# A recurrence's output written with its axes swapped, in strips of 32 columns

## The chip, the cores and the metric

The kernel runs on one core of a Trainium2 chip. The metric is the time of one execution on the device in microseconds; the number given for a kernel is the median of its runs. A core has a matmul engine (TensorE, PE in the rows; its weight loads are shown apart as PEld), a vector engine (VectorE, DVE), ScalarE (ACT), GpSimd (POOL), and SyncE (SP), which here only issues transfers. Each engine works through its own list of instructions in order and waits on semaphores of the others. Matmuls write to PSUM, from which DVE and ACT read.

## The reference

A linear recurrence runs per batch and head over 768 steps, with a state of 48 x 48; its output goes through two feed-forward layers.

```python
for t in range(S):                                  # B, H, S, D = 4, 8, 768, 48
    cur = np.einsum('bhd,bhe->bhde', u[None] * kt, vt)
    y[:, :, t] = np.einsum('bhd,bhde->bhe', rt, state + cur)
    state = wt[:, :, :, None] * state + np.einsum('bhd,bhe->bhde', kt, vt)
...
x = y.transpose(0, 2, 1, 3).reshape(B * S, H * D)    # 3072 x 384
h = x @ w_in                                         # 384 -> 2048
x = (h * np.clip(h + 3.0, 0.0, 6.0) / 6.0) @ w_out   # 2048 -> 384
out = ((x @ w1) * (x @ w2) @ w3) @ w_out2            # 384 -> 1024 -> 1024 -> 384
```

## The kernel before

The 768 steps are cut into six chunks of C = 128. A unit is one chunk of one batch, so there are 24 units, numbered uu = 4 * chunk + batch. Heads go in NP = 4 pairs: head 2 pr on partitions 0 to 47 and head 2 pr + 1 on partitions 64 to 111 (G = 112). All of a unit's products are f32 matmuls; the feed-forward matmuls (`mm3`, three per product: high by high, high by low, low by high) use f32r halves and 512 moving columns.

A unit's steps have one letter each, and the table ORDER is a list of them: `P12` is step P of unit 12. The steps that matter here:

- `P`, `F`: scans over w on DVE. `K` / `k`: k times a decay, on DVE / GpSimd. `R` / `r`: r times a decay, on DVE / GpSimd; both then load the next w.
- `n`, `m`: transposes of k (line 288) and their copy `kn`. `s`: the scores, 8 matmuls of 48 rows, by turns on partitions 0 to 47 and 64 to 111 (line 300). `a`, `b`: copies of the scores to `A` on ACT. `c`, `d`: the causal mask on GpSimd (line 311).
- The bonus, the term with u. First chunk: `q` (GpSimd, line 315) multiplies k and r, `e` (line 321) reduces over d with `ubk`, a 112 x 8 copy of u, and `w` (DVE, line 325) multiplies v by the result. Later chunks: `u`, `v`, `l`, and `w` on GpSimd (line 332). In both cases the product is written over r in the tile `nat`, which holds r, k, v of the unit in rows by time (`nr`, `nk`, `nv`).
- `T`, `t`, `y`: the state's decay, its matmuls (line 341: kn by 96 columns of v per pair) and the addition into `St`.
- `o`: the output (line 354). Per pair one matmul of r by the state (128 x 128 weights, 96 columns) and one per head of `A` by v (48 columns), into `py`, 128 time steps by 384 features.
- `x`: DVE adds the bonus to `py` into `x` (line 368). `f`: three transposes of `x` (line 374) into `px`, 384 features by 128 time steps. `g`, `h`: the high half `xh` on ACT and the low half `xl` on DVE, the operands of the feed-forward layer.

Letters without a number are the feed-forward layer and its weights: `G` and `B` are the matmuls into and out of the hidden layer (9 each), `E M H L` the work between them on ACT, DVE, ACT and GpSimd; `S a d i p` load a block of weights and split it (ACT and DVE), `V` stores; `D` is a dummy matmul, 128 x 256 in bf16, on no data of the problem. A block of the feed-forward layer takes 512 time steps, those of the four units of a chunk, and 16 times `G ... B`. ORDER covers five of the six blocks; the sixth, the fold of w3 into w_out2 and the second layer come after the last unit.

The first transfers stand in LO, in which `w0` is w of unit 0 and `n0` is its `nat`. SyncE issues them; LO1 says how many come before the other instructions of the start. `ubk` is loaded between them, by ScalarE's queue:

```python
for x in LO.split()[0:LO1]:
    LD[x[0]](int(x[1]))
nc.scalar.activation(out=ones, in_=ones, func=ACTF.Copy)
nc.scalar.dma_start(out=ubk[0:G], in_=uT)
```

## Time and profile before

| | us |
|---|---|
| median of 3 runs (907.05 to 911.94) | 910.64 |
| the profiled execution | 910.93 |
| its span, first to last instruction | 909.2 |
| PE busy in the span | 879.9 (97%) |
| DVE, ACT, POOL busy | 376.7, 328.5, 367.4 |

The times in the sections below are of the profiled execution, counted from the start of its span. A matmul's record runs from its start to the modelled end of its results; records of neighbours overlap, so what a matmul costs is read from one start to the next and not from its duration. An f32 matmul stands as two records. The granted clock (PEclk) is given as a share of full speed. "Idle before" is the time in which an engine waited ahead of an instruction, with what released it.

### The profile page before, as it was taken

How to read it: one execution, taken by the hardware profiler on the slowest of the kernel's cores; microseconds unless marked ns; L12 is line 12 of the kernel's file. 1: busy time of each engine (PE TensorE's matmuls, PEld its weight loads, DVE VectorE, ACT ScalarE, POOL GpSimd, SP SyncE). 2: the span in 40 equal slices, each digit the busy share in tenths (PEclk: the TensorE clock that was granted, in tenths of full speed). 3: DMA queues.
4: the chain of work that ended last, by engine and by line, in shares of the span. 5: the costliest groups of instructions: out<-in, count | busy, mean ns of one | idle time of the engine just before them, and what ended most of it. 6: DMA issues, size and time to landing. Idle time of an engine off the chain costs nothing. (4 is left out here: it accounts for less than half of the span.)

```text
span 909.2 us, 11518 instructions
## 1 busy us (share of the span) xinstructions
PE 879.9 (97%) x4534; PEld 731.6 (80%) x4534; DVE 376.7 (41%) x562; ACT 328.5 (36%) x556; POOL 367.4 (40%) x336
## 2 busy tenths in 40 slices
PE   5989999999999999999999999989999999999997
PEld 4978787888888888888888889868888888888785
DVE  5598997634256416544211444246211122112110
ACT  1356653333333333333223655365222222222211
POOL 5376674545546545655322310122323231322221
PEclk6799999999999999999999999999999999999999
DMA  7466531411122113112200445272020403030001
GB/s 211 150 206 196 178 131 58 128 56 59 46 79 81 57 56 93 57 57 82 73 1 1 145 164 165 82 246 73 0 90 1 151 1 132 20 104 28 35 1 39
DMA packets 29230, 80.20 MB, mean 88 GB/s; under 512 B 3312, under 2 KB 3952, under 8 KB 29168
## 3 DMA queue, kind: packets, MB, share of 16 engines
q1 hardware_dynamic: 29040, 79.38, 27.1%
q8 instruction: 38, 0.62, 0.3%
q14 instruction: 24, 0.20, 0.1%
q10 hardware_dynamic: 128, 0.00, 0.0%
HBM read 69.93 MB, written 9.44 MB: 87 GB/s over the span
## 5 line engine op out<-in xcount | busy, mean ns | idle before, releaser
L440 POOL TENSOR_TENSOR gl<-t,gh 128x512 fp32r<-128x512 f32 x144 | 188.7, 1310 | 421.4 <-ACT gh L436 415.6
L436 ACT ACTIVATE gh<-t 128x512 fp32r<-128x512 f32 x144 | 90.9, 632 | 201.6 <-DVE t L595 105.4
L595 DVE TENSOR_TENSOR t<-t,wk 128x512 f32<-128x512 f32 x48 | 32.9, 686 | 200.0 <-PE wk L183 200.0
L429 DVE SCALAR_TENSOR_TENSOR t<-t,h 128x512 f32<-128x512 f32 x96 | 65.4, 682 | 119.7 <-ACT t L424 119.2
L424 ACT ACTIVATE t<-h 128x512 f32<-128x512 f32 x96 | 57.0, 594 | 157.7 <-PE h L183 150.7
L181 PE MATMUL h<-xh,wioh 128*128 128x512 f32 x234 | 97.3, 416 | 0.0
L181 PE MATMUL acc<-gh,wioh 128*128 128x512 f32 x234 | 93.7, 401 | 0.0
L183 PE MATMUL h<-xh,wiol 128*128 128x512 f32 x234 | 92.7, 396 | 0.0
L182 PE MATMUL h<-xl,wioh 128*128 128x512 f32 x234 | 92.3, 394 | 0.0
L182 PE MATMUL acc<-gl,wioh 128*128 128x512 f32 x234 | 91.4, 391 | 0.7 <-POOL gl L440 0.7
L183 PE MATMUL acc<-gh,wiol 128*128 128x512 f32 x234 | 91.6, 391 | 0.0
L594 ACT ACTIVATE t<-h 128x512 f32<-128x512 f32 x48 | 28.6, 595 | 99.9 <-PE h L183 99.9
L182 PE MATMUL acc<-gl,w34h 128*128 128x512 f32 x144 | 56.3, 391 | 0.0
L183 PE MATMUL acc<-gh,w34l 128*128 128x512 f32 x144 | 56.3, 391 | 0.0
L181 PE MATMUL acc<-gh,w34h 128*128 128x512 f32 x144 | 56.2, 390 | 0.0
L362 PE MATMUL wk<-nat,A 128*128 128x48 f32 x384 | 54.9, 272 | 0.2 <-POOL A L311 0.2
L311 POOL TENSOR_SCALAR_AFFINE_SELECT A<-A 128x512 f32<-128x512 f32 x48 | 41.7, 891 | 29.2 <-ACT A L307 29.2
L183 PEld LDWEIGHTS h<-xh,wiol 128*128 128x128 f32 x234 | 44.2, 189 | 10.2
L181 PEld LDWEIGHTS h<-xh,wioh 128*128 128x128 f32 x234 | 44.4, 190 | 9.8 <-DVE t L429 0.3
L165 ACT ACTIVATE z<-st 128x768 f16<-128x768 bf16 (+2 forms) x46 | 41.2, 900 | 30.4 <-DVE st L169 11.7
L182 PEld LDWEIGHTS acc<-gl,wioh 128*128 128x128 f32 x234 | 44.1, 189 | 9.8 <-POOL gl L440 1.0
L183 PEld LDWEIGHTS acc<-gh,wiol 128*128 128x128 f32 x234 | 43.9, 188 | 9.8
(141 smaller groups left out, 1805.8 us busy)
## 6 DMA issues: line engine op xcount, KB each, us to landing
st<-in_wio_dram SPq DMA_DIRECT2D x16, 768.0 KB, 4.3
nat<-in_rkv_dram SPq DMA_DIRECT2D x20, 576.0 KB, 3.8
st<-in_w3T_dram SPq DMA_DIRECT2D x16, 512.0 KB, 4.2
W<-in_wT_dram SPq DMA_DIRECT2D x24, 224.0 KB, 2.7
K<-in_kT_dram SPq DMA_DIRECT2D x24, 224.0 KB, 2.6
R<-in_rT_dram SPq DMA_DIRECT2D x24, 224.0 KB, 2.6
st<-in_wT_dram SPq DMA_DIRECT2D x12, 448.0 KB, 6.6
x1d<-ev SPq DMA_DIRECT2D x18, 256.0 KB, 2.9
```

The source lines that it names most:

```text
L165: nc.scalar.activation(out=z.bitcast(FP16).rearrange("p (n two) -> p n two", two=2)[:, :, 1], in_=half, func=ACTF.Copy)
L181: nc.tensor.matmul(ps_ap, lh, rh, start=first, stop=False)
L182: nc.tensor.matmul(ps_ap, lh, rl, start=False, stop=False)
L183: nc.tensor.matmul(ps_ap, ll, rh, start=False, stop=last)
L311: nc.gpsimd.affine_select(out=A, in_=A, compare_op=ALU.is_ge, fill=0.0, base=-1, pattern=[[0, NP], [1, C]], channel_multiplier=-1)
L362: nc.tensor.matmul(py[:, h * D:(h + 1) * D], d["A"][:, pr, h2, :], d["nv"][:, h, :], start=(h == 0 and first), stop=(h == H - 1), skip_gro ...
L424: nc.scalar.activation(out=t, in_=hp[:, 0:N1], func=ACTF.Relu, bias=3.0)
L429: nc.vector.scalar_tensor_tensor(t, t, 6.0, hp[:, 0:N1], op0=ALU.min, op1=ALU.mult)
L436: nc.scalar.activation(out=gh, in_=t, func=ACTF.Copy)
L440: nc.gpsimd.tensor_tensor(gl, t, gh.bitcast(F32), op=ALU.subtract)
L594: nc.scalar.activation(out=a, in_=pp[0][:, 0:N2], func=ACTF.Copy)
L595: nc.vector.tensor_tensor(a, a, pp[1][:, 0:N2], op=ALU.mult)
```

## The change

`nat` keeps r and k but gets v in another form: two runs, even heads and odd heads, with 64 columns per head. An even head lies at columns 0 to 47 of its 64, an odd one is shifted by 16, and the rest is zero. The three steps `o`, `x`, `f` become one, `o`. It writes `px` directly, features by time: the features are cut into twelve strips of 32, and strip q goes to partitions 32 * (q mod 4) and up, at columns of block q // 4. For each strip the 32-column piece of the state, of the bonus, and of v is the weights, and r, the identity and `A` are the moving operand of 128 columns. Strip 3 pr + 1 holds 16 features of each head of a pair, so it takes two matmuls of v. The bonus is added by the matmul with the identity, in the same accumulation. Bonus and state matmuls read and write the same elements through other patterns. `ubk` is loaded by SyncE after the first LO1 loads, LO1 goes from 4 to 2, and LO and ORDER are new tables: two multiplications by r (`r6`, `r7`) stand on GpSimd and one by k (`K4`) on DVE, and 54 dummies stand where 44 did.

```diff
@@ nat's load
-            t = wt.tile([128, 3, H, D], F32, tag="nat", name="nat", bufs=3)
-        q0 = 2 if uu < B else 0
-        nc.sync.dma_start(out=t.rearrange("p a h d -> p a (h d)")[:, q0:], in_=rkv[uu * C:(uu + 1) * C, q0:])
-        U[uu].update(nr=t[:, 0], nk=t[:, 1], nv=t[:, 2])
+            t = wt.tile([128, 2 * DM + VW], F32, tag="nat", name="nat", bufs=3)
+        q0, q1 = 2 * DM if uu < B else 0, 2 * DM + NP * 128
+        nc.sync.dma_start(out=t[:, q0:q1], in_=rkv[uu * C:(uu + 1) * C, q0:q1])
+        heads = lambda a: a.rearrange("p (h d) -> p h d", d=D)
+        v = t[:, 2 * DM:]
+        U[uu].update(nr=heads(t[:, 0:DM]), nk=heads(t[:, DM:2 * DM]), v64=v[:, 0:NP * 128].rearrange("p (j a e) -> p j a e", j=2, e=64),
+                     nv=v.rearrange("p (j x) -> p j x", j=2)[:, :, 0:NP * 64].rearrange("p j (a e) -> p j a e", e=64)[:, :, :, 0:D])
@@ bonus (the first chunk's on DVE has the same form)
-            nc.gpsimd.tensor_tensor(d["nr"], d["nv"], d["al"].unsqueeze(2).to_broadcast([128, H, D]), op=ALU.mult)
+            nc.gpsimd.tensor_tensor(paired(d["nr"]), d["nv"], wide(d["al"]), op=ALU.mult)
@@ state
-                nc.tensor.matmul(d["pu"][0:G, ds], d["kn"][:, pr, :], flat(d["nv"])[:, ds],
+                nc.tensor.matmul(d["pu"][0:G, ds].rearrange("p (j e) -> p j e", j=2), d["kn"][:, pr, :], d["nv"][:, :, pr, :],
@@ outputs
-            py = d["py"] = pst("wk")
+            px = d["px"] = pst("wk")
+            seen = set()
+
+            def strip(q, lhs, rhs):
+                m, j = divmod(q, 4)
+                nc.tensor.matmul(px[32 * j:32 * j + 32, m * C:(m + 1) * C], lhs, rhs, start=j not in seen, stop=False, skip_group_check=True)
+                seen.add(j)
+
+            if not first:
+                for q in range(3 * NP):
+                    pr, i = divmod(q, 3)
+                    strip(q, St[b][0:G, pr, 32 * i:32 * i + 32], rh[0:G, pr, :])
+            for q in range(3 * NP):
+                strip(q, flat(d["nr"])[:, 32 * q:32 * q + 32], ident)
+            for q in range(3 * NP):
+                pr, i = divmod(q, 3)
+                strip(q, d["v64"][:, i // 2, pr, (0, 32, 32)[i]:(32, 64, 64)[i]],
+                      d["A"][:, pr, i // 2])
             for pr in range(NP):
-                if not first:
-                    nc.tensor.matmul(py[:, pr * 2 * D:(pr + 1) * 2 * D], rh[0:G, pr, :], St[b][0:G, pr, :],
-                                     start=(pr == 0), stop=False, skip_group_check=True)
-                for h2 in range(2):
-                    h = 2 * pr + h2
-                    nc.tensor.matmul(py[:, h * D:(h + 1) * D], d["A"][:, pr, h2, :], d["nv"][:, h, :],
-                                     start=(h == 0 and first), stop=(h == H - 1), skip_group_check=True)
+                strip(3 * pr + 1, d["v64"][:, 1, pr, 0:32], d["A"][:, pr, 1])
             load_r(after(uu))
-
-        def add_x():
-            d["x"] = wt.tile([128, DM], F32, tag="x", name="x")
-            nc.vector.tensor_tensor(d["x"], flat(d["nr"]), d.pop("py")[:, 0:DM], op=ALU.add)
             release("n", uu)
-
-        def x_t():
-            px = d["px"] = pst("wk")
-            for m in range(KM):
-                nc.tensor.transpose(px[:, m * 128:(m + 1) * 128], d["x"][:, m * 128:(m + 1) * 128], ident)
@@ the start
+        nc.sync.dma_start(out=ubk[0:G], in_=uT)
         nc.scalar.activation(out=ones, in_=ones, func=ACTF.Copy)
-        nc.scalar.dma_start(out=ubk[0:G], in_=uT)
@@ tables
-    LO1 = 4
+    LO1 = 2
-    LO = 'w0 k0 r0 w1 k1 r1 w2 r2 n0 k2 w3 n3 k3 r3 n1 n2 s0'
+    LO = 'w0 k0 r0 w1 k2 r1 w3 k1 n0 n3 r2 w2 k3 n1 r3 n2 s0'
-        'P0 F0 q0 K0 D D D D D D D D D D D D D D e0 R0 q1 P1 D D s0 e1 a0 b0 c0 n0 K1 m0 d0 F1 q2 D D D D D o0',
+        'P0 F0 q0 K0 D D D D D D D D D D D D D D e0 R0 P1 D D s0 n0 a0 q1 F1 b0 m0 c0 D D D D D e1 w0 d0 K1 D',
...
```

On PE a unit's output, well inside the stretch in which feed-forward matmuls run without a gap, reads as follows before (line 358 is r by the state, 362 A by v, 374 the transposes of x, 288 those of k; R_105 and St_122 are buffers of r and of one batch's state):

```order
L183 MATMUL acc<-gh,wiol 128x512
L358 MATMUL wk<-St_122,R_105 128x96
L362 MATMUL wk<-nat,A 128x48 x2
...
L181 MATMUL h<-xh,wioh 128x512
L182 MATMUL h<-xl,wioh 128x512
...
L374 MATMUL wk<-ident,x 128x128 x3
L288 MATMUL wk<-ident,K_103 128x112 x4
```

and after (line 369 is the strip's matmul, 292 the transposes of k):

```order
L184 MATMUL acc<-gh,wiol 128x512
L369 MATMUL wk<-R_105,St_122 32x128 x12
L369 MATMUL wk<-ident,nat 32x128 x12
L369 MATMUL wk<-A,nat 32x128 x16
L292 MATMUL wk<-ident,K_103 128x112 x4
L182 MATMUL h<-xh,wioh 128x512
```

Twelve matmuls and, two feed-forward steps later, three transposes became forty matmuls in one place.

On PE the start, behind the first fourteen dummies, reads before (line 321 is the reduction with ubk, 819 a dummy):

```order
L321 MATMUL acc<-ubk,q_117 128x2 x4
...
L300 MATMUL wk<-R_105,K_103 128x128 x8
L321 MATMUL acc<-ubk,q_118 128x2 x4
L288 MATMUL acc<-ident,K_103 128x112 x4
L819 LDWEIGHTS ident
L819 MATMUL h<-ident 128x256
...
L362 MATMUL wk<-nat,A 128x48 x8
```

and after (325 is the reduction with ubk, 304 the scores, 348 the state, 830 a dummy):

```order
L325 MATMUL acc<-ubk,q_117 128x2 x4
...
L304 MATMUL wk<-R_105,K_103 128x128 x8
L292 MATMUL acc<-ident,K_103 128x112 x4
L830 LDWEIGHTS ident
L830 MATMUL h<-ident 128x256
...
L325 MATMUL acc<-ubk,q_118 128x2 x4
...
L369 MATMUL wk<-ident,nat 32x128 x12
L369 MATMUL wk<-A,nat 32x128 x16
L348 MATMUL acc<-nat,kn 112x96 x4
```

The reduction for unit 1 moved behind the transposes of unit 0, and the state matmul of unit 0 follows its output at once.

On the transfer queue of SyncE the start reads before:

```order
L215 DMA W_101<-in_wT_dram 112x512
L215 DMA K_103<-in_kT_dram 112x512
L215 DMA R_105<-in_rT_dram 112x512
L215 DMA W_102<-in_wT_dram 112x512
L215 DMA K_104<-in_kT_dram 112x512
L215 DMA R_106<-in_rT_dram 112x512
L215 DMA W_110<-in_wT_dram 112x512
```

and after:

```order
L216 DMA W_101<-in_wT_dram 112x512
L216 DMA K_103<-in_kT_dram 112x512
L815 DMA ubk<-in_uT_dram 112x8
L216 DMA R_105<-in_rT_dram 112x512
...
L216 DMA K_104<-in_kT_dram 112x512
L236 DMA nat<-in_rkv_dram 128x512
...
L216 DMA W_110<-in_wT_dram 112x512
```

ubk, which ScalarE issued, stands third; w of unit 2 (W_110) went from the seventh place to the thirteenth.

## Rows read from the trace of the kernel before

**Rows 1.** Busy time by stretch (engines, instructions), granted clock, DMA share, GB/s

```profile
50.00:100.00 50.00, 45.98 (x261) 37.80 (x258) 46.52 (x58) 30.08 (x45) 35.35 (x28) 0.97 0.61 196
100.00:150.00 50.00, 47.83 (x278) 39.58 (x277) 46.90 (x58) 23.45 (x36) 33.00 (x29) 1.00 0.38 120
250.00:300.00 50.00, 50.00 (x296) 41.73 (x294) 28.18 (x46) 16.14 (x29) 30.17 (x30) 1.00 0.24 73
650.00:700.00 50.00, 50.00 (x218) 40.68 (x217) 5.50 (x8) 12.87 (x22) 14.11 (x11) 1.00 0.13 41
```

The engines stand in the order PE, PEld, DVE, ACT, POOL.

**Rows 2.** The same view, at the start

```profile
10.00:20.00 10.00, 5.51 (x32) 4.91 (x33) 6.75 (x13) 1.09 (x2) 2.73 (x2) 0.50 0.92 260
20.00:30.00 10.00, 10.00 (x56) 9.29 (x57) 3.97 (x9) 1.10 (x3) 5.24 (x6) 0.50 0.24 70
```

**Rows 3.** Timeline of PE around one output: start, us, engine, line, operation

```profile
211.19 0.40 PE L183 MATMUL acc<-gh,wiol 128*128 128x512 f32 x1
211.42 0.36 PE L358 MATMUL wk<-St,R 112*128 112x96 f32 x2
211.62 0.57 PE L362 MATMUL wk<-nat,A 128*128 128x48 f32 x4
...
214.02 0.47 PE L181 MATMUL h<-xh,wioh 128*128 128x512 f32 x1
214.34 0.39 PE L182 MATMUL h<-xl,wioh 128*128 128x512 f32 x1
```

**Rows 4.** Timeline of PE around one unit's transposes of x

```profile
215.95 0.40 PE L183 MATMUL h<-xh,wiol 128*128 128x512 f32 x1
216.19 0.49 PE L374 MATMUL wk<-ident,x 128*128 128x128 f32 x3
...
216.75 0.40 PE L182 MATMUL acc<-gl,wioh 128*128 128x512 f32 x1
```

**Rows 5.** Timeline of PE around one unit's scores

```profile
205.79 0.39 PE L183 MATMUL acc<-gh,wiol 128*128 128x512 f32 x1
206.11 1.16 PE L300 MATMUL wk<-R,K 48*128 48x128 f32 x16
...
207.54 0.39 PE L182 MATMUL h<-xl,wioh 128*128 128x512 f32 x1
```

**Rows 6.** Timeline of the start, from several engines

```profile
1.74 0.42 SPq L215 DMA_DIRECT2D R<-in_rT_dram  x1
...
6.47 1.90 POOL L315 TENSOR_TENSOR q<-K,R 112x512 f32<-112x512 f32 x1 [1.22 <-DMA R<-in_rT_dram]
...
7.96 0.38 ACTq L805 DMA_DIRECT2D ubk<-in_uT_dram  x1
...
14.48 1.84 PE L321 MATMUL acc<-ubk,q 112*128 112x2 f32 x8 [9.88 <-DMA ubk<-in_uT_dram]
...
50.49 0.47 PE L181 MATMUL h<-xh,wioh 128*128 128x512 f32 x1
```

**Rows 7.** The scores' line: its first 0.1 us (PE, PEld); durations, minimum/median/maximum

```profile
206.10:206.20 0.10, 0.09 (x2) 0.09 (x2) 1.00 0.00 0
...
L300 PEld LDWEIGHTS wk<-R,K x32: 182/188/188, 206.1 to 233.0; 48*128 48x128 f32 x32
L300 PE MATMUL wk<-R,K x32: 272/272/373, 206.1 to 233.1; 48*128 48x128 f32 x32
```

**Rows 8.** PE's groups from 150 to 500 us, A by v

```profile
L362 PE MATMUL wk<-nat,A 128*128 128x48 f32 x240 | 34.2, 265 | 0.0
```

**Rows 9.** DVE's groups from 40 to 150 us: busy us, mean ns, idle before

```profile
L280 DVE TENSOR_TENSOR R<-R,W 112x512 f32<-112x512 f32 x7 | 6.4, 919 | 0.0
L274 DVE TENSOR_TENSOR K<-K,P 112x508 f32<-112x508 f32 x4 | 4.9, 1220 | 0.0
L368 DVE TENSOR_TENSOR x<-nat,wk 128x384 f32<-128x384 f32 x6 | 3.2, 536 | 0.0
```

**Rows 10.** Weight loads of one column: durations in ns, minimum/median/maximum

```profile
L636 PEld LDWEIGHTS wk<-ok,ones x2: 79/80/82, 854.1 to 854.1; 128*1 128x1 f32 x2
```

More of the change, by code (lines that the diff above doesn't have):

```diff
@@ L59 @@
     PAD = 16
+    VW = 2 * (NP * 64 + 16)
     N1 = B * C
@@ L197 @@
     Rb += [ep.tile([128, FL], F32, name=f"R{q}") for q in (2, 3)]
-    nat3 = ep.tile([128, 3, H, D], F32, name="nat3")
+    nat3 = ep.tile([128, 2 * DM + VW], F32, name="nat3")
     qT = [ep.tile([128, FL], F32, name=f"q{q}") for q in range(2)]
@@ L322, in q_alpha @@
                                  start=(pr == 0), stop=(pr == NP - 1), skip_group_check=True)
+        paired = lambda t: t.rearrange("p (a j) d -> p j a d", j=2)
+        wide = lambda t: t.rearrange("p (a j) -> p j a", j=2).unsqueeze(3).to_broadcast([128, 2, NP, D])
         def q_bonus():
-            nc.vector.tensor_tensor(d["nr"], d["nv"], d.pop("pl")[:, 0:H].unsqueeze(2).to_broadcast([128, H, D]), op=ALU.mult)
+            nc.vector.tensor_tensor(paired(d["nr"]), d["nv"], wide(d.pop("pl")[:, 0:H]), op=ALU.mult)
         def alpha():
@@ L394, in unit @@
             "V": lambda: V_.tensor_tensor(d["nr"], d["nr"], d["nk"], op=ALU.mult),
-            "q": q_t, "e": q_alpha, "l": alpha, "w": q_bonus if first else bonus, "T": decay, "t": state, "y": state_add, "o": outputs, "x": add_x, "f": x_t,
+            "q": q_t, "e": q_alpha, "l": alpha, "w": q_bonus if first else bonus, "T": decay, "t": state, "y": state_add, "o": outputs,
             "g": lambda: x_split(0), "h": lambda: x_split(1)}
@@ L935, in _layout @@
     rows = lambda a: a.reshape(a.shape[0] // 128, 128, a.shape[1]).transpose(1, 0, 2)
-    d = {"rkv": np.ascontiguousarray(
-        np.stack([r, k, v]).reshape(3, B, H, S // C, C, D).transpose(3, 1, 4, 0, 2, 5)).reshape(B * S, 3, H * D)}
+    nat = lambda a: a.reshape(B, H, S // C, C, D).transpose(2, 0, 3, 1, 4).reshape(B * S, H, D)
+    rkv = np.zeros((B * S, 2 * H * D + H * 64), np.float32)
+    rkv[:, 0:H * D] = nat(r).reshape(B * S, -1)
+    rkv[:, H * D:2 * H * D] = nat(k).reshape(B * S, -1)
+    v64 = rkv[:, 2 * H * D:].reshape(B * S, 2, H // 2, 64)
+    v64[:, 0, :, 0:D] = nat(v)[:, 0::2]
+    v64[:, 1, :, 16:16 + D] = nat(v)[:, 1::2]
+    d = {"rkv": rkv}
     d.update({n + "T": pairs(a, n == "w") for n, a in (("r", r), ("k", k), ("v", v), ("w", w))})
```

59 rows, old and new, of the table ORDER are left out of this document.

## The prediction

> **What bounds the kernel now.** I read the busy time by stretches first. From 150 us on the matmul engine is the bound: 50.0 of 50 us busy with the vector engine at about half of that [rows 1]. Between 50 and 150 us matmul and vector engine are both above 90% and either can be the limit. Before that neither is: matmuls run at a granted clock of 0.50, the lower of the two levels, from 10 to 30 us [rows 2]. So a microsecond taken from the matmul stream after 150 us is a microsecond of the end; before, it must be asked what is late instead. Second, I read the matmul stream record by record where a unit's output is inserted between feed-forward matmuls [rows 3 to 5]. Third, the start [rows 6]: the matmul engine stands still for 9.9 us until 14.48 us, waiting for ubk, and issues its first feed-forward matmul at 50.49 us.
>
> All times are of the profiled execution, 910.9 us with a span of 909.2; the median shown, 910.64, is 0.3 lower, and the sum is corrected by that.
>
> **Part 1, the output of a unit on the matmul engine.** What an insertion costs is the time from the feed-forward matmul before it to the second one behind it, less two feed-forward steps of 50/218 = 0.229 us [rows 1]. The output: 214.34 - 211.19 - 0.46 = 2.69 us [rows 3]. The transposes of x: 216.75 - 215.95 - 0.46 = 0.34 us [rows 4]. Together 3.03 us. These 12 matmuls appear as 24 records, so each f32 matmul is two passes.
>
> After, there are 40 matmuls (12 of state, 12 of bonus, 16 of A and v), so 80 passes of 128 moving columns, no transposes, and ten matmuls in each of four groups of 32 columns of the array. No row shows column groups. The nearest are the scores, two row halves of 48 rows side by side: two loads and two matmuls stand in the first 0.1 us although each lasts longer [rows 7], and the 16 passes run from 206.11 to 207.27 [rows 5]. The last starts a median duration, 0.27 [rows 7], before that end: 0.89 us from first start to last, that is one exposed load and seven steps, or 8 slots of 0.111 us for 16 passes. Two halves run wholly side by side. The insertion costs 207.54 - 205.79 - 0.46 = 1.29 us [rows 5], so 0.40 us goes for filling and emptying the array around the change of form.
>
> I take four groups side by side as two are: 20 slots x 0.111 + 0.40 = 2.62 us against 3.03, so **0.41 us less per unit**. Fifteen units stand behind 150 us (240 records of 16 each [rows 8]): **-6.2 us**. Upwards the bound is no overlap at all, 80 x 0.111 = 8.9 us; downwards the slot can hardly shrink, as 128 columns take 0.11 in the transposes also (three in 0.49 us, the last lasting 0.27 [rows 4, 7]). I choose the row of the scores since it is the same f32 form, alternating tiles, in the same place of the stream. For the likeliest case a slot of 0.109 to 0.125 gives -6.8 to -2.
>
> **Part 2, the vector engine between 50 and 150 us.** The add into x goes: six of 0.54 us in the window from 40 to 150 us, 3.2 us. Two multiplications of R go to GpSimd (2 x 0.92 = 1.8) and one of K comes back (1.2) [rows 9]. Net 3.8 us less on an engine that is 93% busy there. GpSimd takes on two multiplications for one and is 68% busy there [rows 1]; I take **-3 us**, bounds -4 and 0, the latter if the matmul engine is the true limit there.
>
> **Part 3, the start.** The first matmul of unit 0 waits for ubk, which ScalarE's queue issues at 7.96 us and which is used at 14.48 [rows 6]. Issued third by SyncE, some 1.7 us in, it no longer ends a wait; then the product q of K and R does, which GpSimd starts at 6.47 and ends at 8.37. R is one place later in the queue, one issue of 0.42. So this matmul comes at 8.8: -5.6 us. Against that: ten more dummy matmuls stand ahead of the first feed-forward one (40 where 30 stood), 0.11 to 0.21 us each, 1.1 to 2.1. The scan and the R product of unit 4 fall behind the first feed-forward matmul and its K product before it, about 1.2 us of vector work left over. W of unit 2 is loaded in the thirteenth place, not the seventh, and the four early v loads grow from 192 to 256 KB, 0.26 MB in a stretch that moves 260 GB/s [rows 2], 1 us. The first units' outputs change little: 14 slots + 0.40 = 1.95 us for 16 passes of 0.11 and the transposes, 2.1, twice that at the lower clock. Net **-3 us**, bounds -6 and +2.
>
> **Hidden parts.** The later loads of r, k and v grow by a ninth; after 150 us DMA is 24% busy [rows 1]. The state matmul has the same columns from two runs of 48; the bonus has the same 384 elements in another pattern. A new wait appears: the strips need the bonus, which only the add needed before. If it is late, all feed-forward matmuls queue behind it. The order puts each bonus well ahead of its output (that of unit 12 before the output of unit 10), so I cost it at nothing; without that cover it would cost up to one GpSimd multiplication per unit.
>
> **Sum.** -6.2 - 3 - 3 = -12.2: 910.9 - 12.2 - 0.3 = **898 us**.
>
> **Rivals.** *No change.* The slot comes to 0.13 us, at which the unit costs 20 x 0.13 + 0.40 = 3.0 as before, and the dummies and later loads eat the start; only part 2 stays: 907 to 908 us. For it: clock and load order at the start are poorly known. Chance 0.15.
>
> *Loads exposed: slower.* The strips share all rows of the array, and each pass must wait for its own load of weights. A load of 1 column takes 0.080 us [rows 10] and one of 128 takes 0.188 [rows 7], so 32 columns take about 0.106 on a straight line, and a slot becomes 0.217: 4.7 us per unit, +1.7. Fifteen units give +26, five between 50 and 150 us +9, where the matmul engine has little room, the first four +5, the start -3: about 947 us. It decides from a slot of (3.03 - 0.40)/20 = 0.131 us for the unit alone, and of 0.146 once the 6 us of parts 2 and 3 over 20 units are set against it. Against it: feed-forward loads, which fill the whole array, lie under running matmuls; weight loads are busy 40.7 of 50 us beside matmuls at 50.0 [rows 1]. Chance 0.11.
>
> [...]
>
> *One after another.* Column groups don't run side by side at all, so the change doesn't do what it says: 80 passes, 8.9 + 0.1 us per unit, +6 for 20 units and +4 for the first four: about +130, near 1040 us. The scores speak against it, though two row halves read different partitions and four column groups the same ones. Chance 0.05.
>
> **How the numbers follow.** The forecast has 0.64, from 888 (all lower bounds, with some more for an earlier rise of the clock) to 908. Another 0.05 lies in slots between 0.13 and 0.2 and in a still larger gain. The range 888 to 922 leaves out the two last rivals and some of the 0.05, 0.19 in all. A measurement of this kernel tells 0.5% from no change, so faster means below 906.1 and slower above 915.2: faster 0.69 (the forecast, and a third of "no change"), same 0.14, slower 0.17.
>
> **What would show it.** Right: 80 strip records per unit in some 2.3 us, four starting almost together, and 2.6 us between the neighbours; no vector adds; the first ubk matmul near 9 us and the first feed-forward matmul near 47; the vector engine's full stretch ending some 6 us sooner, near 142; matmuls without gaps after. Wrong: strips in pairs or singly, slots above 0.131 us, a first feed-forward matmul not before 50 us, matmuls waiting for the bonus, or a half clock that lasts longer than before.

## The result and the profile after

The changed kernel takes **886.55 us** (median of 4 runs, 884.49 to 888.7) against 910.38 of the kernel before on the same chip (4 runs). The ratio is 0.9743, 95% interval 0.9702 to 0.9784, so it gains 19.7 to 27.1 us. 898 was forecast, with 888 as the low end: the sign was right, and the gain is nearly twice the one forecast. The profiled execution took 888.7 us, the longest of the four, with a span of 887.0 us.

Busy time by stretch (answers to [rows 1]; engines in the order PE, PEld, DVE, ACT, POOL, then granted clock, DMA share, GB/s):

```profile
50.00:100.00 50.00, 48.15 (x451) 37.98 (x449) 47.16 (x57) 30.51 (x44) 35.68 (x30) 1.00 0.59 195
100.00:150.00 50.00, 48.20 (x380) 38.85 (x381) 39.16 (x59) 22.72 (x37) 40.89 (x34) 1.00 0.36 119
250.00:300.00 50.00, 50.00 (x446) 41.02 (x437) 26.59 (x45) 16.14 (x28) 28.53 (x28) 1.00 0.27 82
...
130.00:140.00 10.00, 9.52 (x42) 7.30 (x41) 9.10 (x14) 4.33 (x8) 8.86 (x8) 1.00 0.24 79
140.00:150.00 10.00, 10.00 (x46) 8.25 (x45) 4.25 (x8) 4.67 (x9) 8.51 (x7) 1.00 0.20 79
```

The matmul engine is still the bound, and the vector engine's full stretch ends some way into 140 to 150 us (4.25 of 10 us busy there). Timeline of PE around one output without other insertions (answers to [rows 3, 4]; start, us, engine, line, operation):

```profile
399.05 0.40 PE L184 MATMUL acc<-gh,wiol 128*128 128x512 f32 x1
399.37 0.86 PE L369 MATMUL wk<-R,St 112*32 112x128 f32 x24
400.05 0.84 PE L369 MATMUL wk<-ident,nat 128*32 128x128 f32 x24
400.71 1.06 PE L369 MATMUL wk<-A,nat 128*32 128x128 f32 x32
401.70 0.50 PE L182 MATMUL h<-xh,wioh 128*128 128x512 f32 x1
402.03 0.39 PE L183 MATMUL h<-xl,wioh 128*128 128x512 f32 x1
```

The 80 passes lie within 401.70 - 399.37 = 2.33 us, and the insertion costs 402.03 - 399.05 - 0.46 = 2.52 us by the prediction's own rule, where output and transposes cost 3.03. Timeline of the start, SyncE's queue and PE (answers to [rows 6]):

```profile
1.74 0.42 SPq L815 DMA_DIRECT2D ubk<-in_uT_dram  x1
...
8.32 1.87 PE L325 MATMUL acc<-ubk,q 112*128 112x2 f32 x8 [3.71 <-POOL q L319]
...
10.57 2.08 PE L304 MATMUL wk<-R,K 48*128 48x128 f32 x16
...
20.67 1.16 PE L304 MATMUL wk<-R,K 48*128 48x128 f32 x16
...
38.99 0.48 PE L182 MATMUL h<-xh,wioh 128*128 128x512 f32 x1
```

The first ubk matmul came 6.2 us sooner and waits for q now, the first feed-forward matmul 11.5 us sooner. The scores tell the matmul rate: 2.08 us at the lower one, 1.16 at the full one.

**Where the time went** is read best from the n-th matmul of the feed-forward layers: all kernels here have the same 3216 (the fold of w3 counted in), and the table gives how many us sooner the n-th starts than in the kernel before (from the start times in the traces; one execution of each). The kernels are those of the next section.

```
n                           1    50   250   500   900  1500  1900  2000  3216
at (us, kernel before)     50    72   138   217   337   510   593   621   902
changed kernel           11.5  19.3  14.8  20.9  23.8  25.2  24.3  22.1  22.1
e1  ubk only              8.1   9.7   9.6   9.5   9.5   9.5   9.5   9.9   9.9
e3  strips only           4.1   8.2   8.5  10.9  13.5  17.1  16.8  14.9  14.9
e3b strips and ubk       12.1  15.8  16.2  18.6  21.2  24.8  24.7  23.0  23.0
e5  no later dummies     10.3  17.1  12.9  19.1  22.0  23.4  23.3  23.5  23.5
e9  dummies moved        -0.4   1.3   1.1   1.1   1.1   1.1   1.3   1.1   1.1
e14 one add moved         2.2   6.5   4.0   4.0   4.0   4.0   3.6   4.0   4.0
e12 loads at hand-over   11.4  19.2  14.6  20.8  23.7  25.1  24.5  28.9  28.9
```

The changed kernel, e5 and e12 have another table of steps than the rest, so their columns between 50 and 900 go up and down against the others'. With strips three stretches matter: a lead of 8 us, with ubk 16 (19 in the new table), is there by 72 us; it grows by about half a microsecond per unit until some 510; and in most executions some 2 us are given back near 570 to 600 us, at the hand-over to the second feed-forward layer. A lead of one execution isn't a median: e1's is the fastest of its six (900.6 us), so its 9.9 stands above the 6.0 of the timed runs.

### The profile page after: what moved, and what is told of

Read it like the earlier page. It is cut to its first block, busy times and chain, and to the rows that moved or that the text cites. A ratio compares the mean times of both kernels' runs of the same rounds, so it can differ in the third digit from the quotient of the medians.

```text
span 887.0 us, 13899 instructions
## 1 busy us (share of the span) xinstructions
PE 865.2 (98%) x5752; PEld 707.5 (80%) x5752; DVE 357.5 (40%) x537; ACT 330.5 (37%) x556; POOL 375.8 (42%) x337
## 4 chain that ended last, share of the span: by engine, by line
PE 78%; issue 12%; POOL 5%; DVE 3%; ACT 1%; DMA 0%; SPq 0%; POOLq 0%; ACTq 0%; DVEq 0%
PE h L182 9%; PE acc L183 9%; PE acc L182 9%; PE acc L184 9%; PE h L184 9%; PE h L183 9%; PE wk L369 5%; PE wk L183 4%; PE wk L184 4%; PE wk L182 4%; POOL gl L451 4%; PE wk L304 3%; PE wk L348 1%; PE wk L292 1%; POOL A L315 1%
## 5 line engine op out<-in xcount | busy, mean ns | idle before, releaser
L451 POOL TENSOR_TENSOR gl<-t,gh 128x512 fp32r<-128x512 f32 x144 | 192.0, 1334 | 390.6 <-ACT gh L447 390.5
L182 PE MATMUL h<-xh,wioh 128*128 128x512 f32 x234 | 94.9, 406 | 0.3 <-DVE t L440 0.3
L182 PEld LDWEIGHTS acc<-gh,wioh 128*128 128x128 f32 x234 | 44.0, 188 | 9.4 <-issue 0.2
L183 PEld LDWEIGHTS h<-xl,wioh 128*128 128x128 f32 x234 | 44.0, 188 | 8.5
```

The costliest lines, as they stand in the source:

```text
L182: nc.tensor.matmul(ps_ap, lh, rh, start=first, stop=False)
L183: nc.tensor.matmul(ps_ap, lh, rl, start=False, stop=False)
L451: nc.gpsimd.tensor_tensor(gl, t, gh.bitcast(F32), op=ALU.subtract)
```

## The experiments

Times are medians; each ratio is to the kernel before on the same chip, with its 95% interval. A gain in us is taken from the ratio, not from two medians.

**The parts, one at a time.** e1 is the kernel before with ubk's load alone moved:

```
-    LO1 = 4
+    LO1 = 2
+    nc.sync.dma_start(out=ubk[0:G], in_=uT)
     nc.scalar.activation(out=ones, in_=ones, func=ACTF.Copy)
-    nc.scalar.dma_start(out=ubk[0:G], in_=uT)
```

> The kernel before with one edit: ubk is loaded third, by SyncE. Theory A (the wait for ubk made the start late, and all behind it moves up by as much): the first ubk matmul comes at 8.3 to 8.8 us instead of 14.48, the first feed-forward matmul at about 44 to 45 instead of 50.49, and the time falls by 5 to 6 us, to about 905. Theory B (the matmul clock rises early only through the dense strips or the new table): the first ubk matmul comes early, but the passes stay at the lower rate until about 30 us, the first feed-forward matmul comes at 47 to 50 and the time falls by at most 2 us, to about 909.

904.33 us, ratio 0.9934 (0.9904 to 0.9963): 6.0 us less (3.4 to 8.8), as theory A has it. e2 is the changed kernel with the same five lines turned back.

> The changed kernel with ubk back on ScalarE's queue and LO1 at 4. Theory A: the first ubk matmul falls back to about 14.5 us, the first feed-forward matmul from 38.99 to about 45, and the time rises by 5 to 6 us, to about 892. Theory B: the strips raise the clock within a few us anyway, the first feed-forward matmul comes at 41 to 42, and the time rises by 2 to 3 us, to about 889.

895.09 us, 0.9832 (0.9804 to 0.986): 8.1 of the changed kernel's 23.4 us are gone, more than either theory said. e3 is the changed kernel with ubk on ScalarE's queue and with the order of steps and of early loads that the kernel before has (the steps x and f taken out, w0 moved ahead of o0): strips alone.

> The strips alone: the changed kernel's output in the order table, load order and ubk queue of the kernel before (steps x and f dropped, the bonus of unit 0 put ahead of its output). Additive sum from the traces: 0.50 us less per unit on the matmul engine behind 150 us (15 units, 7.5) and about 3 us of vector adds in the middle: about 900. Theory A: the first feed-forward matmul stays at 48 to 50 us, since the ubk wait is there. Theory B: the strips raise the clock sooner, the first feed-forward matmul comes at 44 to 46, and the time is about 895.

895.89 us, 0.9842 (0.9814 to 0.987): 14.4 us less, near theory B. e3b is e3 with ubk third on SyncE's queue.

> The same with ubk loaded third by SyncE, so that only the order table and the load order of the kernel before are left. If the three parts add up: 5 to 6 us less than the strips alone, about 894, and the new table is worth the 7 us left to the changed kernel's 886.6. Rival (the table only fits the strips and is worth nothing by itself): within 2 us of the changed kernel, 886 to 889.

887.73 us, 0.9753 (0.9724 to 0.9781): the rival. Timelines of PE, first ubk and first feed-forward matmul, of e1 and then of e3:

```profile
8.37 1.87 PE L321 MATMUL acc<-ubk,q 112*128 112x2 f32 x8 [3.87 <-POOL q L315]
...
42.42 0.47 PE L181 MATMUL h<-xh,wioh 128*128 128x512 f32 x1
```

```profile
15.01 1.84 PE L325 MATMUL acc<-ubk,q 112*128 112x2 f32 x8 [10.40 <-DMA ubk<-in_uT_dram]
...
46.37 0.47 PE L182 MATMUL h<-xh,wioh 128*128 128x512 f32 x1
```

So ubk is worth 6.0 us alone and 8.1 beside the strips (e2, and e3b against e3), which the intervals don't tell apart, and the strips 14.4; the two together in the old order (e3b, 22.5) reach the changed kernel (23.4) within the intervals. The new order of steps and loads, with its ten more dummies, is worth nothing that can be measured.

**What makes the strips run side by side.** In e4 the same 40 matmuls come one column group after the other within the state, the bonus and the A-times-v matmuls, so that three of one group stand in a row; in e7 they come two groups at a time:

```
-  for q in range(3 * NP):
+  for q in sorted(range(3 * NP), key=lambda q: q % 4):                        # e4
+  for q in sorted(range(3 * NP), key=lambda q: (q % 4 // 2, q // 4, q % 2)):  # e7
```

> The changed kernel with the same 40 strip matmuls per unit in another order: within the state, the bonus and the A-times-v matmuls, all strips of column group 0 first, then those of group 1, 2 and 3. Neighbours in TensorE's queue then share a group of columns nearly always. Theory (four passes run side by side because the queue brings a strip of another group each time): the passes of one group follow each other at 0.107 us and a group can overlap the next only at its ends, so about 68 slots of 0.107 plus 0.40, some 7.7 us per unit where 2.53 stood; 15 units behind 150 us alone give 78 us, all of them about 110 to 130: 990 to 1015 us in all. Rival (the engine reorders strips for itself, or the 29 ns per record of the changed kernel are a rate of issue that does not ask which group a strip belongs to): still about 2.5 us per unit and 887 us.

915.75 us, 1.0062 (1.0042 to 1.0081). The output alone costs 3.93 us, neither the 7.7 of one theory nor the 2.5 of the other. Timeline of PE in e4:

```profile
237.27 0.40 PE L184 MATMUL acc<-gh,wiol 128*128 128x512 f32 x1
237.59 1.26 PE L369 MATMUL wk<-R,St 112*32 112x128 f32 x20
238.59 0.30 PE L369 MATMUL wk<-ident,nat 128*32 128x128 f32 x1
238.66 0.30 PE L369 MATMUL wk<-R,St 112*32 112x128 f32 x2
238.72 0.27 PE L369 MATMUL wk<-ident,nat 128*32 128x128 f32 x1
...
241.32 0.60 PE L292 MATMUL wk<-ident,K 112*128 112x112 f32 x4
```

The first bonus strip (ident, nat; group 0) starts at 238.59, ahead of state strips (R, St; groups 2 and 3) that stand before it in the queue. So here a strip started ahead of strips of other groups that were to come first. How far ahead a strip can go was not tried; the 80 passes start within 241.32 - 237.59 = 3.73 us, so 2.3 of them ran at once on average, by an estimate from 0.109 us a pass (the step from four passes to the next four in the changed kernel).

> The changed kernel with its strips in the order of pairs of column groups: all strips of groups 0 and 1 in turn, then those of groups 2 and 3. With all strips of one group in a row an output cost 3.93 us, not the 7.7 of passes that keep their order: in that trace passes of up to three groups ran beside each other although they stood six passes apart in the queue. Theory (the engine lets a later strip of another group go ahead of the queue, a few matmuls deep): two groups at a time fill most of the four, the output costs 2.6 to 3.2 us, 15 units and the five before give 889 to 900. Rival (a strip only overlaps the one or two ahead of it): two groups run, the slot is twice as wide, the output costs 4.5 us and the time is about 925.

891.34 us (two runs), 0.9799 (0.977 to 0.9829); the output costs 2.76 us, as the first theory of the two has it. Against 2.52 for four in turn that is 0.24 us more per unit, some 5 us over twenty units by estimate, and the time is about as much above the changed kernel's. So the slot of the prediction's first part comes from column groups that run side by side.

**Whether dummies and vector engine set the pace.** e5 leaves out the dummy matmuls of the table behind the first fourteen.

> The changed kernel without the dummy matmuls behind the first fourteen (those between the steps of the first units in the table). The forecast charged the ten more dummies with 1.1 to 2.1 us at the start. Theory now (the matmul engine waits for the vector engines there and the dummies lie in its idle time, so they cost nothing by their length): if they do nothing else either, the first feed-forward matmul stays within 1 us of 38.99 and the time within 2 us of 886.6. Rival A (as forecast, they stand in the way): about 40 dummies at 0.11 to 0.21 us give 4 to 8 us back at the first feed-forward matmul, some 35 us, and a time of 879 to 883. Rival B (the busy engine is what lets its clock rise, and the strips and dummies are why it rose at 19.5 us): without them matmuls keep the lower pitch longer, the first feed-forward matmul comes 2 to 6 us later and the time is 889 to 893.

886.3 us, 0.9725 (0.9708 to 0.9743): no difference. Some 5.7 us of dummies (by the starts of the steps around them in the changed kernel) ahead of the first feed-forward matmul are gone, and yet it comes at 40.23, 1.2 us later; the rate goes up and down until 42.5 us (the twelve bonus strips of a unit take 1.51 us at 29.96 and 0.86 at 34.79, a feed-forward matmul 0.63 us at 42.09 and 0.40 at 42.81). The time that rival A saves and the lower rate of rival B both show, and B's share is the larger: the lead is 1.8 us smaller at the 1500th matmul. What lets the rate rise e5 does not show. That the times are the same in the end is luck of the hand-over, at which this execution loses nothing (23.3 to 23.5) and the changed kernel's 2.2 us. e6 issues the subtraction for the low half of x twice:

```
+  nc.vector.tensor_tensor(xl, pxv, xh.bitcast(F32), op=ALU.subtract)
   nc.vector.tensor_tensor(xl, pxv, xh.bitcast(F32), op=ALU.subtract)
```

> The changed kernel with one vector instruction of 128 x 384 per unit given back: the subtraction that makes the low half of x is issued twice into the same tile, 24 times some 0.55 us. Theory of the forecast's second part (between 50 and 150 us the vector engine is the limit, and the add that went is worth its length there, 3 us): the feed-forward matmuls done by 150 us fall by about 13 of 0.23 us, and the time is 889 to 890. Rival (the matmul engine is the limit there and the vector engine only keeps pace): no change, 886 to 887.5, and as many feed-forward matmuls by 150 us.

888.29 us, 0.9757 (0.9732 to 0.9783), between the two forecasts; the interval overlaps with the changed kernel's, and in the traces 345 feed-forward matmuls have started by 150 us in both. The vector engine's length is no limit there.

**What was won by 72 us.** The prediction's second part goes by busy shares; it doesn't use PE's waits in the kernel before between 45 and 160 us (waiter, releaser: us in total, times, longest), nor this place of its timeline:

```profile
PE wk L374 <- DVE x L368: 4.3, 3, 3.3
```

```profile
65.33 0.52 PE L374 MATMUL wk<-ident,x 128*128 128x128 f32 x3 [3.33 <-DVE x L368]
...
66.57 0.63 PE L181 MATMUL h<-xh,wioh 128*128 128x512 f32 x1
```

The transposes wait for the vector engine's add into x, and behind the longest of these waits eight feed-forward matmuls run at the lower rate (0.63 us long where 0.39 is usual; the granted clock is 0.57 from 66 to 70 us). With the strips neither add nor transposes are left. e14 takes that longest wait alone out of the kernel before, by one step of its table:

```
-  ... o4 T5 E K5 i L M p a v5 n4 B H d S m4 L x4 i t4 ...
+  ... o4 T5 E K5 i L M x4 p a v5 n4 B H d S m4 L i t4 ...
```

> The kernel before with one edit in its table: the vector engine's add into x of unit 4 stands ahead of the split of a weight tile instead of behind it and eight other steps. In the trace of before the matmul engine's transposes of that x wait 3.33 us for this add, until 65.33 us, since the vector engine's queue is in order and the split, 5.39 us long there, stands ahead; right behind the wait nine feed-forward passes run at the lower rate (66.2 to 69.5 us). The strips have neither add nor transposes, so both would go with them. Theory (that is the 4.1 us that the strips with the old table gained between the first and the 50th feed-forward matmul): the wait falls below 1 us, the lower rate behind it goes, and the 50th feed-forward matmul comes 3 to 5 us sooner than at 72 us; the time 906 to 908. Rival (the split is then late by as much and its reader, a feed-forward matmul, waits instead): the 50th within 1 us of 72, the time 910 to 912.

908.34 us, 0.9988 (0.9974 to 1.0002). PE's wait for the add in the same stretch of e14:

```profile
PE wk L375 <- DVE x L369: 1.1, 3, 0.8
```

It fell from 4.3 to 1.1 us, and the lead grows by 4.3 us between the first and the 50th matmul, as it does by 4.1 for the strips alone; but 2.5 of that are gone by the 250th, and the timed runs show 1.1 us, not 2 to 4. (The lead of 2.2 at the first matmul has nothing to do with the edit: ubk came 0.6 us sooner in this execution, and the rate did not fall near 36 us: the scores at 34.58 take 1.16 us, those at 35.35 in the kernel before 2.03.) e9, the next experiment, leaves this place as it is. Its rate did not fall behind the same wait (0.40 us a matmul there), and its lead too grows, by 1.7 us between the first and the 50th matmul, of which 1.5 are left at the 250th; in e14 1.8 are left. So what lasts is mostly the slow stretch behind the wait, which one execution has and another has not. That the wait itself costs the kernel anything is not shown.

e9 and e15 ask for the rate at the start, in the kernel before: e9 moves nine dummies from behind c1 to behind o0, the first output; e15 puts twenty strips on constants there in place of them.

```
-  ... D D D D D o0 w0 R1 e2 P2 s1 a1 F2 k2 b1 x0 q3 c1 D D D D D D D D D f0 ...
+  ... D D D D D o0 D D D D D D D D D w0 R1 e2 P2 s1 a1 F2 k2 b1 x0 q3 c1 f0 ...  # e9
+  ... D D D D D o0 Q w0 R1 e2 P2 s1 a1 F2 k2 b1 x0 q3 c1 f0 ...                  # e15
   # Q: for q in range(20): j = q % 4
   #    nc.tensor.matmul(pw[32*j:32*j+32, 0:128], ident[:, 32*j:32*j+32], ident, ...)
```

> The kernel before with one edit in its table: the nine dummy matmuls that stand behind c1 are moved to stand behind o0, the output of unit 0. No work is added or taken. In the trace of before the matmul engine's passes keep the lower rate until 32.0 us and fall to it again from 35.4 to 38.8; in every kernel with strips the rate rises at or within 2 us of the end of the first unit's strips. Theory (part of what the strips gave at the start is an earlier rise of the clock, and a stretch of dense passes behind the first output is enough for it): the rate rises by 28 us, the ubk matmuls and scores of units 1 and 2 then take half the time, the first feed-forward matmul comes 2 to 4 us sooner than 50.49, and the time is 907 to 909. Rival (the rise has to do with the strips themselves, or the early work is bound by the vector engine): the first feed-forward matmul within 1 us of 50.49, time 910 to 911.5.

912.78 us, 1.0025 (1.0009 to 1.004): slightly slower. Timeline of PE in e9, then of e15:

```profile
25.76 2.12 PE L819 MATMUL h<-ident 128*128 128x256 bf16 x9
...
29.31 2.08 PE L300 MATMUL wk<-R,K 48*128 48x128 f32 x16
...
50.94 0.48 PE L181 MATMUL h<-xh,wioh 128*128 128x512 f32 x1
```

```profile
26.12 2.36 PE L824 MATMUL h<-ident 128*32 128x128 f32 x40
...
30.21 2.08 PE L300 MATMUL wk<-R,K 48*128 48x128 f32 x16
...
39.38 2.08 PE L300 MATMUL wk<-R,K 48*128 48x128 f32 x16
...
54.91 0.47 PE L181 MATMUL h<-xh,wioh 128*128 128x512 f32 x1
```

> The kernel before with the nine dummy matmuls behind c1 replaced by twenty f32 strips of 32 columns on constants, in four column groups side by side, behind o0, the output of unit 0: the form of pass that the changed kernel has there, and about the same time on the matmul engine (40 passes, some 2.2 us at the lower rate). Nine dummies of the whole array at that place left the rise of the rate at 32 us. Theory (four strips side by side are what brings the rate up within 2 us in all kernels with strips): the scores of unit 1, 2.02 us in the trace of before, take 1.1 to 1.6 here, the rate has risen by 30 us, and the first feed-forward matmul comes 1 to 4 us before 50.5. Rival (the rise comes a fixed time behind the first ubk matmul at 14.5 us, or with the work that follows, whatever stands there): the scores of unit 1 take 2.0, the first feed-forward matmul 50 to 51.

913.18 us, 1.0029 (1.0013 to 1.0046). The theories of both fall: the scores behind dummies and strips take 2.08 us, the lower rate. e9's first feed-forward matmul comes within 0.5 us of 50.49, as its rival has it, though its time lies above the rival's. In e15 the rate stays down longer than in e9 and in the kernel before (the third set of scores still takes 2.08 us at 39.38; the next set of the kernel before, at 41.54, takes 1.16, and e9's third, at 35.91, 1.64), and the first feed-forward matmul comes 4.4 us later than before, which neither side had. The form of the strips alone does not bring the rate up. The earlier rise goes with the real strips: the second unit's scores take 1.16 us with them in the changed kernel, e3 and e5, and 2.08 without them in the kernel before, e1, e9, e14 and e15. What in them brings it stays open.

**The hand-over to the second layer.** Timelines of PE and of ScalarE in the changed kernel, and the longest of the waits of SyncE's queue between 535 and 570 us (waiter, releaser: us in total, times, longest):

```profile
568.83 0.39 PE L184 MATMUL acc<-gh,wio2l 128*128 128x512 f32 x1
572.82 0.79 PE L182 MATMUL acc<-gh,wio2h 128*128 128x512 f32 x1 [3.61 <-ACT gh L447]
...
575.20 0.63 PE L182 MATMUL acc<-gh,wio2h 128*128 128x512 f32 x1
```

```profile
569.89 1.06 ACT L166 ACTIVATE z<-st 128x768 f16<-128x768 bf16 x1 [8.33 <-DMA st<-in_w_dram]
```

```profile
SPq L582 <- PE wk L184: 18.3, 1, 18.3
```

The matmul engine waits 3.61 us for a gelu that stands in ScalarE's queue behind a conversion, which waits for its weights; then it runs at the lower rate until 579.0 (0.63 us a matmul; the granted clock is 0.57 from 575 to 580 us). The kernel before waits there too, 2.01 us, and keeps its rate (0.39 us a matmul). e8 puts a `yield` behind the first two loads of `w12_ticks`, so that the conversion comes one step later than its load.

> The changed kernel with the first two weight loads of the second layer's conversion issued one step of its table earlier, so that more feed-forward work lies between the load and ScalarE's instruction that reads it. In the changed kernel ScalarE stands for 8.3 us at 569.9 us waiting for that load, the matmul engine waits 3.6 us for ScalarE's gelu behind it, and from 572.4 to 579.3 us the granted clock is down in the rows (0.57 in the stretch 575 to 580). Theory (this wait is where 3.5 of the 25.7 us that the change had gained by 500 us were given back): ScalarE's wait shrinks to under 2 us, the clock stays up, and the time is 882 to 884.5. Rival (the wait moves to the next reader of weights, or the load has to wait for a buffer that comes free no sooner): 886 to 888 with the wait at the same place or some us later.

889.77 us, 0.9762 (0.974 to 0.9784): not better, the lead falls to 20.0. The last row above says why: on SyncE's queue the residual's load (L582) waits 18.3 us for its space to come free, and the weight loads behind it start no sooner for a `yield` (561.96 us, where it was 561.75). The wait for the gelu falls to 1.96 us, but the conversion is later by its step, and the matmul engine then waits 2.37 us for converted weights. e11 puts 26 dummies ahead of the matmul that waits.

> The changed kernel with 26 dummy matmuls (about 0.11 us each, 2.8 us) in the matmul engine's queue ahead of the feed-forward matmul at 572.82 us, which waits 3.61 us for ScalarE's gelu and behind which the passes keep the lower rate until 579.0. The dummies read constants and no one reads them. Theory (the 2.9 us of lead given back at the hand-over are the half rate behind the wait and not the wait, which before has too with 2.01 us): no pass of the lower rate near 575, the lead over before stays near 24 us to the end and the time is 883.5 to 885. Rival (the rate falls for another reason, or the chain on ScalarE, not the matmul engine, sets the pace there): 886 to 887.5.

886.0 us, 0.9735 (0.9715 to 0.9755). In its trace no pass near 575 us has the lower rate (0.39 to 0.50 us a matmul, granted clock 1.00 from 570 to 580 us) and the lead falls by 1.1 us, not 2.2; but the timed runs can't tell it from the changed kernel, so the rival's number came out. e12 moves the loads past the one that waits:

```
         load(0)
         load(1)
+        yield
...
-                    load_x1(0)
                     wl = w12_ticks()
+                    next(wl)
+                    load_x1(0)
```

> The changed kernel with the first two weight loads of the second layer's conversion issued ahead of the load of the residual x1 (768 KB, 6.5 us to landing), which stands ahead of them on SyncE's queue now. ScalarE's conversion waits 8.33 us for the first of these loads until 569.89 us, and the relu and gelu that the matmul engine waits for stand behind that conversion. Theory (the residual's load takes the bandwidth and the place of the load that is waited for): the conversion starts 2 to 4 us sooner, the matmul engine's wait of 3.61 us falls to 0 to 1.6, the lower rate behind it is gone, the time is 883 to 885. Rival (the order of two loads that share the engines hardly moves the first's end, or the residual is then late and its split holds up the first matmuls of the second layer): 886 to 889.

**881.63 us** (five runs, 881.02 to 881.75), 0.9684 (0.9664 to 0.9704): below the lowest run of the changed kernel. SyncE's queue in e12:

```profile
542.50 4.10 SPq L151 DMA_DIRECT2D st<-in_w_dram  x2
560.80 0.62 SPq L583 DMA_DIRECT2D x1r<-x1d  x1
```

The loads go out from 542.50, not from 561.75 us, the matmul engine no longer waits for the gelu (0.23 us from one start to the next up to 573.8 us), and the lead rises to 28.9 us, since the wait that the kernel before has there is gone too. Of the two reasons in the expectation the place in the queue is the one that shows, 19 us in the start of the load; what sharing the bandwidth cost beside it was not tried by itself.

> The two edits at the hand-over together: the weight loads ahead of the residual's, and the 26 dummies ahead of the feed-forward matmul that waits. If the wait is gone by the first edit, the dummies stand in the way of about 2.8 us less what is left of the wait: 884 to 887. If the first edit does nothing, this runs as the dummies alone, 883.5 to 885.

884.48 us, 0.9721 (0.9701 to 0.9741): with no wait left, the dummies stand in the way of their 2.8 us. e12 beats both kernels by itself.

## Why the prediction was off

**Part 1, right in mechanism, mis-sized.** Four groups of columns run side by side: the slot is (2.52 - 0.40)/20 = 0.106 us where 0.111 was taken, and a unit saves 0.51 us (0.56 with the transposes of K behind it), not 0.41. The 0.40 is what the scores' insertion has left over; that it goes for filling and emptying the array was my reading, which no run shows. Over 15 units that is about 8 us, not 6.2; e3's lead grows by 8.6 us between the 250th and the 1500th matmul, where sixteen outputs lie. The slot that I took as hardly able to shrink did shrink a little: by the starts in the traces four passes follow four in 0.109 us, where two of the scores follow two in 0.112, and the first step is 0.134 us, in the scores 0.213. The rivals of exposed loads (947) and of one strip after another (1040) are out by the same row, and "no change" with them. The loads of one output take what the first of these rivals put them at, 0.106 us (durations in ns, minimum/median/maximum):

```profile
L369 PEld LDWEIGHTS wk<-R,St x24: 106/110/110, 399.4 to 399.9; 112*32 112x32 f32 x24
```

But they lie under passes of other strips that run meanwhile: the strips share all rows, and in a slot of 0.106 us four passes are done, each with a load that takes as long as the slot.

**Part 2, near in number by luck, wrong in reason.** -3 us was put on the vector engine's busy time. e6 gives 0.55 us per unit back and no feed-forward matmul is lost, so length was not what counted. The strips alone win 4.4 us between the first and the 250th matmul (4.1 to 8.5). Between e1 and e3b, which differ by the strips alone as well, it is 2.6 (4.0 to 6.6), as e1's rate did not fall behind the same wait (3.33 us until 57.12, 0.39 us a matmul behind it). Four units' outputs lie in that stretch, and at 0.51 us each they make 2.0 us by estimate: the saving of part 1, which the forecast counted only behind 150 us. The wait view of the kernel before has PE standing 4.3 us for the add, but by e14 and e9 little of what lasts can be put down to it.

**Part 3, the step that failed.** The start was put at -3 us net, with the first feed-forward matmul 3.5 us sooner; it came 11.5 us sooner. Ubk alone was put at -5.6 us and measures -6.0 (e1), beside the strips -8.1: that line stands, down to the new waiter, q. The set-offs of 3.3 to 4.3 us behind it do not (and -5.6 with them makes -1.3 to -2.3, not -3). Ten more dummies were charged by their length, but by e5 the dummies there give back in rate at least what they take in time (some 5.7 us of them gone, the first feed-forward matmul 1.2 us later); the later load of unit 2 and the left-over steps of unit 4 cost nothing that can be measured, as e3b with the old table equals the changed kernel within the intervals. And strips were taken to change little in the first units, 14 slots against 16 passes: e3's first feed-forward matmul comes 4.1 us sooner than before's, and e3b's 4.0 sooner than e1's. In the trace of the kernel before the matmul engine shows no wait between the first ubk matmul (14.48) and 50.49 us, so its work and its rate set this stretch: three sets of scores run at the lower rate before (2.08, 2.08 and 2.03 us at 16.70, 27.33 and 35.35), one in the changed kernel (2.08 us at 10.57). "Some more for an earlier rise of the clock" stood in the range and had no part in the sum. That the rise comes sooner with strips is shown by the second unit's scores (1.16 us against 2.08); why it does stays open.

**Not in the forecast: what is given back.** Between the 1500th matmul and the end the strips alone lose 2.2 us of their lead and the changed kernel 3.1, most of it at the hand-over, where the longest wait of the matmul engine is 1.6 us longer than before and the lower rate follows it. "Matmuls without gaps after" held only until there. It is not in every execution: e5's longest wait there is 1.83 us, its rate stays up (granted clock 1.00 from 570 to 580 us), and its lead is kept.

**Sum.** Ubk 6.0 to 8.1 (5.6 forecast, less set-offs), strips 14.4 by e3 against 9.2 for parts 1 and 2. By the leads of e3 the 14.9 are 4.1 ahead of the first feed-forward matmul, 4.4 up to the 250th, 8.6 in the units behind, less 2.2 at the hand-over. The low end of 888 holds the lower bounds of the three parts (6.8, 4 and 6 us) and 5.8 us more, which had no sum of their own. The profiled execution, 888.7 us, lies just inside it and the median 1.5 us below: the start took nearly all of those 5.8 us, and part 1 went beyond its bound.

**Hidden parts.** The new wait for the bonus was costed at nothing; between 45 and 160 us it is there once (waiter, releaser: us in total, times, longest):

```profile
PE wk L369 <- POOL nat L339: 1.3, 1, 1.3
```

1.3 us in all: small, as said, but not nothing. The longer v loads show nowhere as a wait of the matmul engine. **What would show it:** strips in 2.33 us (2.3 said), the first four within 0.02 us of one another, 2.52 between neighbours (2.6), first ubk matmul at 8.32 (9), the vector engine's full stretch ending between 140 and 150 (142) were right; the first feed-forward matmul at 38.99 (47) and the gaps at the hand-over were not.

## What to carry to other kernels

Before an edit is priced by an engine's busy share, read who waits for the removed instruction, and then test what the wait is worth: an add of 0.55 us held up the matmul stream for 3.3, yet taking that wait out gained 1.1 us, which can't be told from nothing. Work saved on the engine that sets the pace counts wherever that engine sets it: the outputs between 50 and 150 us were left out of the forecast. Four f32 passes that fill 32 columns each took 0.109 us together here when four column groups were fed in turn; two groups at a time cost 0.24 us more per unit, one at a time 1.4. A result that comes out transposed saves the add's copy and the transposes behind it. When a change makes an early part faster, look at the next hand-over for a load whose issue waits in a queue behind one that can't start yet; here moving two loads past it was worth about a fifth of the whole change.

## What the runs showed of the hardware

- TensorE started strips of 32 columns out of the order of its queue: with three matmuls of one column group in a row (e4) the output took 3.93 us, where 80 passes in sequence would take 8.9 by 0.111 us each, and a bonus strip started at 238.59 us, ahead of a state strip at 238.66 that stands before it. So these strips did not start in the order of the list, which the description ahead of the prediction gives for every engine.
- The rate of the first 20 us can't be read from the granted clock of the view by stretches alone: in the changed kernel it stands at 1.00 from 0 to 20 us while the scores at 10.57 take 2.08 us, and 1.16 at 20.67. The duration of a known group is the safer reading.

```profile
10.00:20.00 10.00, 10.00 (x98) 8.17 (x99) 9.69 (x14) 1.66 (x4) 6.73 (x7) 1.00 1.05 293
```

- The rate fell (0.63 us a feed-forward matmul) behind a wait of 3.61 us at the hand-over of the changed kernel and behind one of 3.33 at 65.33 us in the kernel before, not behind one of 2.01 at the hand-over there (0.39). But in e9 the same wait of 3.33 us at 65.62 was followed by passes at the full rate (0.40), and in e8 the rate fell at 574.85 us (0.63) behind waits of 1.96 and 0.93 us at the hand-over. So in these traces the length of the wait doesn't tell whether the rate falls; the traces of e9 and of the kernel before differ by it at the same place of the table.
- With the matmul engine's passes unbroken, the lower rate lasted from 14.9 to beyond 41 us in e15 (the scores at 39.38 still take 2.08 us). The passes put behind the first output were expected to end it in e9 and in e15, and ended it in neither; which work does is open.
